# Tokens as the stationary side of the second product: a batch's 576 tokens as four blocks of 128, with 64 left over

## The chip, the cores and the metric

The kernel runs on one core of one Trainium2 chip. The core has TensorE (PE in the profile, its weight loads PEld), VectorE (DVE), ScalarE (ACT), GpSimd (POOL) and SyncE (SP), which here only issues transfers. The metric is device time in microseconds (us) of one execution, lower is better.

## The reference

Eight batches of 576 tokens. In each of 8 heads of 64, 32 learned positions `p` attend to the tokens, and the tokens then attend to what that packed. The heads side by side are `x` with 4608 rows of 512, and a two-layer network with a leaky activation follows:

```python
def _ref(q, k, v, p, w_in, w_out, alpha):
    p_packed = sm_attn(p, k, v)
    x = sm_attn(q, p_packed, p_packed)      # 4608 x 512, float32
    h = x @ w_in                            # 512 x 2048
    g = np.maximum(h, 0.0) + alpha * np.minimum(h, 0.0)
    return g @ w_out                        # 2048 x 512
```

## The kernel before

Everything is held transposed: features on the partitions, tokens along the columns. A number that must be exact is split into a high and a low part of type fp32r, and a product is made of three matmuls (high by high, high by low, low by high).

The hidden width 2048 is cut into `NF` = 16 slices `f` of 128. `pieces` lists stretches of tokens: half batches of 288 for batches 0 to 5, and for the last two batches 320, 512 (256 of each) and 320. For one piece `k` and one `f`:

- `first(k, f)` (lines 702 to 739) makes the hidden slice in PSUM, `ps_h`. From batch 1 on that is six matmuls of the piece's width (lines 724 to 726). The packed `w_in` of the batch comes from `split_pw`, which splits 256 columns at a time on ACT and POOL (lines 694, 695). Then the activation: ACT (731), DVE (732), and the split of the result into `gh` (ACT, 737) and `gl` (DVE, 738), two buffers each.
- `second(k, f)` (lines 741 to 786) multiplies by `w_out`. A 128 x 128 block of `w_out` is stationary and the piece's tokens move: 4 blocks of output features x 3 matmuls = 12 matmuls of the piece's width (line 757), into the accumulators `acc0` to `acc3`, one PSUM bank each. At `f` = 15 each bank is copied out by DVE or ACT (783, 781) and stored by SP (786).

The loop at the end of the kernel runs through `order`: at step i it calls `first` of entry i and `second` of entry i - 2 (`AHEAD` = 2). Between these it lets generators go on by a step: the attention of coming batches (lines 244 to 507), the conversion of the weights, and `packed_w` (642), which makes the packed `w_in` of a coming pair of batches, its weights loaded by SP into the three buffers of pool `win` (line 650). `plan` says from which step on each generator runs. Batches 0 and 1 go in sweeps over parts of `f` (`part`); from entry 64 on (batch 2) each piece runs through all 16 slices. A scheduler reorders instructions within what their data allow, so the order on an engine isn't that of the text. Attention with `hold` set would wait for a step; `2 * g - 2 >= 6` never holds with eight batches.

## Time and profile before

| | |
|---|---|
| median of 3 runs | 791.69 us (790.46, 791.77, 791.69) |
| span of the profiled execution, first to last instruction | 790.0 us (the profile gives no other time of it) |
| PE, PEld busy | 97%, 91% |
| ACT, DVE, POOL busy | 69%, 59%, 45% |
| TensorE's granted clock, by 40ths of the span | 9 tenths or more of full speed throughout |
| DMA | 91.68 MB, mean 116 GB/s |

Busy time of PE counts pipelined matmuls with modelled ends, so that two neighbours overlap: the cost of a matmul in a stream is the distance from its start to the next one's, which the timeline shows. Idle time of an engine that isn't the limit costs nothing.

### The profile page before, as it was taken

Reading aid. Unit: us, or ns where it says so; the run is one execution under the profiler, and the core shown is the slowest. Engines: PE = TensorE matmul, PEld = TensorE weight load, DVE = VectorE, ACT = ScalarE, POOL = GpSimd, SP = SyncE. Lnnn points to the kernel's source line nnn. Section 1 sums busy time; section 2 is a strip of 40 time slices with the busy share of each in tenths; the row PEclk is TensorE's granted clock in tenths of the full one; section 3 lists DMA queues with packets and bytes.
Section 4 is the critical chain, followed back from the end, with each engine's and each line's share of the span. In section 5 each row is a group of like instructions: output and inputs, shape, how many; then the busy total and the mean of one; then the engine's idle time right before and its main releaser. Section 6 shows DMA issues by size and latency. Waiting matters only on the chain.

```text
span 790.0 us, 14895 instructions
## 1 busy us (share of the span) xinstructions
PE 766.6 (97%) x5168; PEld 715.6 (91%) x5168; DVE 464.1 (59%) x1070; ACT 543.3 (69%) x1242; POOL 359.2 (45%) x391
## 2 busy tenths in 40 slices
PE   6789999999999999999999999999999999999998
PEld 4567668999999899999999999999999999988898
DVE  3989988776857435557654265576663343432433
ACT  4788789776777887677768776777678644534343
POOL 2003306563777755678764155676632222333220
PEclk9999999999999999999999999999999999999999
DMA  9787775121363774232225621321037100000100
GB/s 317 258 259 256 242 223 156 46 64 46 104 197 121 263 239 152 75 91 76 79 88 186 231 89 46 91 61 46 1 92 244 42 32 1 34 1 1 49 6 34
DMA packets 59035, 91.68 MB, mean 116 GB/s; under 512 B 5200, under 2 KB 35920, under 8 KB 58960
## 3 DMA queue, kind: packets, MB, share of 16 engines
q1 hardware_dynamic: 58384, 90.33, 35.9%
q8 instruction: 41, 0.67, 0.4%
q10 hardware_dynamic: 576, 0.40, 0.2%
q14 instruction: 34, 0.28, 0.1%
HBM read 68.69 MB, written 22.02 MB: 115 GB/s over the span
## 4 chain that ended last, share of the span: by engine, by line
PE 83%; ACT 8%; DVE 4%; DMA 3%; issue 1%; ACTq 0%; DVEq 0%; SPq 0%
PE acc L757 47%; PE ps_h L724 7%; PE ps_h L725 7%; PE ps_h L726 7%; PE ps_h L713 3%; DMA wraw<-in_w_in 2%; PE ps_m L386 2%; PE ps_m L224 2%; PE ps_m L225 2%; PE ps_m L673 1%; PE ps_m L671 1%; PE ps_m L672 1%; DVE mag L140 1%; ACT pw L639 1%; PE acc L215 1%
## 5 line engine op out<-in xcount | busy, mean ns | idle before, releaser
L757 PE MATMUL acc<-gh,wo 128*128 128x288 f32 (+2 forms) x1920 | 331.1, 306 | 3.1 <-ACT gh L737 2.9
L757 PEld LDWEIGHTS acc<-gh,wo 128*128 128x128 f32 x1920 | 283.3, 188 | 19.8 <-ACT gh L737 6.2
L695 POOL TENSOR_TENSOR pwl<-pw,pwh 128x512 fp32r<-128x512 f32 (+1 forms) x128 | 148.2, 1164 | 220.6 <-ACT pwh L694 155.6
L732 DVE SCALAR_TENSOR_TENSOR ps_h<-neg,nal,ps_h 128x288 f32<-128x288 f32 (+2 forms) x240 | 129.1, 539 | 156.2 <-ACT neg L731 155.3
L757 PE MATMUL acc<-gl,wo 128*128 128x288 f32 (+2 forms) x960 | 197.3, 308 | 0.0
L738 DVE TENSOR_TENSOR gl<-ps_h,gh 128x288 fp32r<-128x288 f32 (+2 forms) x240 | 113.7, 474 | 88.3 <-ACT gh L737 85.4
L757 PEld LDWEIGHTS acc<-gl,wo 128*128 128x128 f32 x960 | 150.5, 188 | 4.8
L737 ACT CAST gh<-ps_h 128x288 fp32r<-128x288 f32 (+2 forms) x240 | 99.7, 416 | 76.9 <-DVE ps_h L732 63.4
L724 PE MATMUL ps_h<-a_h,pwh 128*128 128x288 f32 (+2 forms) x448 | 133.7, 298 | 0.0
L725 PE MATMUL ps_h<-a_l,pwh 128*128 128x288 f32 (+2 forms) x448 | 132.3, 295 | 0.0
L726 PE MATMUL ps_h<-a_h,pwl 128*128 128x288 f32 (+2 forms) x448 | 132.3, 295 | 0.0
L731 ACT ACTIVATE neg<-ps_h 128x288 f32<-128x288 f32 (+2 forms) x240 | 102.3, 427 | 39.5 <-PE ps_h L726 31.0
L694 ACT CAST pwh<-pw 128x512 fp32r<-128x512 f32 (+1 forms) x128 | 70.8, 567 | 64.9 <-PE ps_h L725 62.0
L188 POOL TENSOR_TENSOR xl<-xraw,xh 128x576 fp32r<-128x576 f32 x48 | 69.8, 1457 | 51.1 <-ACT xh L187 44.3
L725 PEld LDWEIGHTS ps_h<-a_l,pwh 128*128 128x128 f32 x448 | 84.4, 188 | 1.3 <-issue 0.2
L724 PEld LDWEIGHTS ps_h<-a_h,pwh 128*128 128x128 f32 x448 | 84.3, 188 | 1.4 <-issue 0.2
L726 PEld LDWEIGHTS ps_h<-a_h,pwl 128*128 128x128 f32 x448 | 84.4, 188 | 0.2
L676 ACT COPY pw<-ps_m 64x512 f32<-64x512 f32 x96 | 55.7, 581 | 7.6 <-PE ps_m L673 6.0
L344 POOL TENSOR_TENSOR vs<-vraw,vs 128x640 fp32r<-128x640 f32 x24 | 37.7, 1573 | 10.7 <-ACT vs L343 8.3
L227 ACT COPY lo<-ps_m 64x288 f32<-64x288 f32 x96 | 37.3, 396 | 6.3 <-PE ps_m L225 4.4
L713 PE MATMUL ps_h<-a_f,pw 128*128 128x288 f32 x128 | 38.1, 420 | 3.1 <-DVE a_f L481 3.1
L187 ACT CAST xh<-xraw 128x576 fp32r<-128x576 f32 x48 | 32.1, 674 | 6.6 <-PE ps_m L224 3.5
(132 smaller groups left out, 920.5 us busy)
## 6 DMA issues: line engine op xcount, KB each, us to landing
w<-w_split SPq DMA_DIRECT2D x32, 512.0 KB, 4.1
xraw<-in_kT SPq DMA_DIRECT2D x32, 288.0 KB, 3.0
xraw<-in_qT SPq DMA_DIRECT2D x32, 288.0 KB, 2.8
vraw<-in_v SPq DMA_DIRECT2D x32, 256.0 KB, 2.9
wraw<-in_w_in SPq DMA_DIRECT2D x16, 512.0 KB, 5.0
wraw<-in_w_out SPq DMA_DIRECT2D x16, 512.0 KB, 4.4
w_split<-w SPq DMA_DIRECT2D x16, 512.0 KB, 2.9
w<-w_whole SPq DMA_DIRECT2D x24, 256.0 KB, 3.5
```

The costliest lines, as they stand in the source:

```text
L188: nc.gpsimd.tensor_tensor(out=xl, in0=raw, in1=fv(xh), op=ALU.subtract)
L694: nc.scalar.copy(out=th[:, w], in_=src)
L695: nc.gpsimd.tensor_tensor(out=tl[:, w], in0=src, in1=fv(th[:, w]), op=ALU.subtract)
L713: nc.tensor.matmul(ps[:, :size], th[:, i, fs], a_f[:, i, t : t + size], start=(i == 0), stop=(i == 1))
L724: nc.tensor.matmul(po, th[:, w, i], a_h[:, i, tok], start=hi, stop=False)
L725: nc.tensor.matmul(po, th[:, w, i], a_l[:, i, tok], start=False, stop=False)
L726: nc.tensor.matmul(po, tl[:, w, i], a_h[:, i, tok], start=False, stop=lo)
L731: nc.scalar.activation(out=neg, in_=x, func=AF.Relu, scale=-1.0)
L732: nc.vector.scalar_tensor_tensor(out=x, in0=neg, scalar=nal[:, f : f + 1], in1=x, op0=ALU.mult, op1=ALU.add)
L737: nc.scalar.copy(out=gh, in_=x)
L738: nc.vector.tensor_tensor(out=gl, in0=x, in1=fv(gh), op=ALU.subtract)
L757: product = nc.tensor.matmul(acc[o][:, :width], wo_t[f][:, half_, os_], g, start=begin and n == 0, stop=end and n == 2,)
```

## The change

Batches 0 and 1 stay as they are. From batch 2 on, `order` alternates between the two halves of a batch at each `f`, and `first` always makes 288 columns. In `second_by_tokens` the token side `g` is stationary (128 tokens) and all 512 columns of `w_out[f]` move: per half batch two blocks of 128 tokens, so 2 x 3 = 6 matmuls of 512 columns into two banks (`acc0`, `acc1` for the first half, `acc2`, `acc3` for the second). The 32 tokens that are left in each half are stored to DRAM (`g_rest`), for each `f` one transfer of 128 x 2 x 32 numbers; at the end of a pair of batches `rest` loads the pair's 128 left-over tokens (four loads of 512 KB into the buffers of `win`) and runs 48 matmuls of 512 columns, into `acc3` or, at the very end, a bank of `ps_m`. For the last four slices of the last batch the left-over tokens are put straight into the loaded tile by POOL.

The output now has tokens on the partitions. `put` turns a bank on DVE in blocks of 32 x 32 and stores it in four transfers of 32 x 16 pieces of 128 bytes. In the last batch `put_turned` copies a bank out (half by ACT, half by DVE), turns it with four PE transposes, copies it out again and stores it. The buffers of the output tile go from 4 to 3, `gh` and `gl` become one tile `g` with four buffers, and `split_pw` splits once per batch and not once per half or piece. `hold` goes away.

```diff
-    op = ctx.enter_context(tc.tile_pool(name="op", bufs=4))
+    op = ctx.enter_context(tc.tile_pool(name="op", bufs=3))
...
+    g_rest = [dram.tile([NJ, P, 4, 2, P], F32, name=f"g_rest{g}") for g in range(1, B // 2)]
...
-        ways = pieces[k]
-        n = 256 // len(ways)
-        h = f * P // n
-        if (k, h) not in pj:
...
+        b, h = k // 2, f // 2
+        own = (b, k % 2 if b < 2 else 0, h)
+        if own not in pj:
+            th = pwj.tile([P, 2, 256], F32R, name="pwh", tag="pwh")
+            tl = pwj.tile([P, 2, 256], F32R, name="pwl", tag="pwl")
+            j, c = h // 2, h % 2 * 256
+            src = pw[b, j][:, :, c : c + 256]
+            nc.scalar.copy(out=th, in_=src)
+            nc.gpsimd.tensor_tensor(out=tl, in0=src, in1=fv(th), op=ALU.subtract)
+            pj[own] = (th, tl)
+        fs = slice(f % 2 * P, f % 2 * P + P)
+        return [t[:, :, fs] for t in pj[own]]
...
-        for b, t, size in ways:
-            for half in range(t // HS, -(-(t + size) // HS)):
...
+        b, t = k // 2, k % 2 * HS
...
+        x = ps_h.tile([P, 512], F32, name="ps_h", tag="h")[:, :HS]
...
-        gh = gp.tile([P, width], F32R, name="gh", tag="gh")
-        gl = gp.tile([P, width], F32R, name="gl", tag="gl")
-        nc.scalar.copy(out=gh, in_=x)
-        nc.vector.tensor_tensor(out=gl, in0=x, in1=fv(gh), op=ALU.subtract)
-        gs[k, f] = (gh, gl)
+        g = gp.tile([P, 2, HS], F32R, name="g", tag="g", bufs=4)
+        nc.scalar.copy(out=g[:, 0], in_=x)
+        nc.vector.tensor_tensor(out=g[:, 1], in0=x, in1=fv(g[:, 0]), op=ALU.subtract)
+        gs[k, f] = g
...
-                nc.scalar.copy(out=part[k][:, o], in_=acc[o][:, :width])
+                nc.scalar.copy(out=part[k][:, o], in_=acc[o][:, :HS])
                 continue
-            if k in part:
-                to = part[k][:, o]
-            elif width > CW:
-                if o % 2 == 0:
-                    two = pwp.tile([P, 2, 512], F32, name="two", tag="pw")
-                to = two[:, o % 2]
...
+            nc.vector.tensor_tensor(out=to, in0=acc[o][:, :HS], in1=to, op=ALU.add)
+            if f == NF - 1:
+                nc.sync.dma_start(out=outT[o * P : (o + 1) * P, b * S + t : b * S + t + HS], in_=to)
+
+    def by_tokens(to, st, f, kept_order=False):
+
+        for n, (i, half_) in enumerate(((0, 0), (0, 1), (1, 0))):
+            product = nc.tensor.matmul(
+                to, st[:, i], wo_t[f][:, half_, :],
+                start=(f == 0 and n == 0), stop=(f == NF - 1 and n == 2),
+            )
+            if kept_order:
+                tc.keep_in_program_order(product)
+
+    def put(of, toks):
+
+        to = op.tile([P, DM], F32, name="ot", tag="ot")
+        nc.vector.transpose(out=to, in_=of)
+        for r, tok in enumerate(toks):
+            nc.sync.dma_start(
+                out=outT[:, tok : tok + 32].rearrange("(c j) i -> j c i", j=32),
+                in_=to[32 * r : 32 * r + 32].rearrange("j (c i) -> j c i", i=32),
+            )
...
+    def put_turned(of, runs, n):
+
+        tag = ("xh", "xl")[n % 2]
+        own = xin.tile([P, S], F32, name="own", tag=tag)[:, :DM].rearrange("t (q o) -> t q o", q=NOC)
+        nc.scalar.copy(out=own[:, : NOC // 2], in_=of[:, : DM // 2])
+        nc.vector.tensor_copy(out=own[:, NOC // 2 :], in_=of[:, DM // 2 :])
+        yield
+        turned = ps_h.tile([P, 512], F32, name="ps_h", tag="h").rearrange("o (q t) -> o q t", q=NOC)
+        to = op.tile([P, NOC, P], F32, name="ot", tag="ot")
+        for q in range(NOC):
+            tc.keep_in_program_order(nc.tensor.transpose(turned[:, q], own[:, q], ident))
+        nc.scalar.copy(out=to[:, : NOC // 2], in_=turned[:, : NOC // 2])
+        nc.vector.tensor_copy(out=to[:, NOC // 2 :], in_=turned[:, NOC // 2 :])
+        n = P // len(runs)
+        for i, tok in enumerate(runs):
+            nc.sync.dma_start(
+                out=outT.rearrange("(q o) t -> o q t", o=P)[:, :, tok : tok + n],
+                in_=to[:, :, i * n : i * n + n],
+            )
+        yield
...
+    def second_by_tokens(k, f):
+        b, hf = k // 2, k % 2
+        if f == 0:
+            for n in range(2):
+                tag = f"acc{2 * hf + n}"
+                acc_t[k, n] = ps_a.tile([P, 512], F32, name=tag, tag=tag)
+        g = gs.pop((k, f))
+        c0, r0 = ((0, 256), (32, 0))[hf]
+        own = slice((2 * (b % 2) + hf) * 32, (2 * (b % 2) + hf) * 32 + 32)
+        left_over = fv(g[:, :, r0 : r0 + 32])
+        if b == B - 1 and f >= NF - 4:
+            if not kept:
+                kept.append(win.tile([P, 4, 2, P], F32R, name="rest", tag="w"))
+                nc.sync.dma_start(
+                    out=fv(kept[0][:, :, :, : P // 2]), in_=g_rest[-1][NJ - 1, :, :, :, : P // 2]
+                )
+            nc.gpsimd.tensor_copy(out=kept[0][:, f % 4, :, own], in_=left_over)
+        else:
+            nc.sync.dma_start(out=g_rest[b // 2 - 1][f // 4, :, f % 4, :, own], in_=left_over)
+        for n in range(2):
+            by_tokens(acc_t[k, n], g[:, :, c0 + n * P : c0 + n * P + P], f, b == B - 1 and f == NF - 1)
+            if f == NF - 1:
+                at_ = b * S + hf * HS + c0 + n * P
+                if b == B - 1:
+                    turns.append(put_turned(acc_t.pop((k, n)), [at_], len(turns)))
+                    next(turns[-1])
+                else:
+                    put(acc_t.pop((k, n)), range(at_, at_ + P, 32))
...
+    def rest(bp, pool, tag):
+
+        to = pool.tile([P, 512], F32, name=f"rest_{tag}", tag=tag)
+        for j in range(NJ):
+            if j == NJ - 1 and kept:
+                st = kept[0]
...
+                st = win.tile([P, 4, 2, P], F32R, name="rest", tag="w")
+                nc.sync.dma_start(out=fv(st), in_=g_rest[bp - 1][j])
+            for f in range(4):
+                by_tokens(to, st[:, f], 4 * j + f, bool(kept) and j > 0)
+            if j == NJ - 1:
+                if kept:
+                    turns.append(put_turned(to, [(2 * bp + i) * S + 256 for i in range(2)], 0))
+                    next(turns[-1])
+                else:
+                    put(to, [(2 * bp + i) * S + 256 + r for i in range(2) for r in (0, 32)])
+            yield
...
-    order += [(k, f) for k in range(4, len(pieces)) for f in range(NF)]
+    order += [(2 * b + hf, f) for b in range(2, B) for f in range(NF) for hf in range(2)]
...
-            plan += [(T + at_n, attention(2 * g + n // 2, n % 2, hold=(None, T + HOLD[n % 2])[n // 2] if 2 * g - 2 >= 6 else None), RG)]
+            plan += [(T + at_n, attention(2 * g + n // 2, n % 2), RG)]
...
-        if i >= AHEAD:
-            second(*order[i - AHEAD])
+        if i < AHEAD:
+            continue
+        k, f = order[i - AHEAD]
+        if k < 4:
+            second(k, f)
+            continue
+        second_by_tokens(k, f)
+        if k % 4 != 3:
+            continue
+        if k < 2 * B - 1:
+            if f == NF - 1:
+                drain(rest(k // 4, ps_a, "acc3"))
+        elif f == NF - 1:
+            for _ in rest(k // 4, ps_m, "m"):
+                drain(turns.pop(0))
+            drain(turns.pop(0))
```

Three places of the program, as the builder orders them. PE first, in the middle of a batch: the second product of one step before (piece of 288; `acc` are the accumulators, `wo` is `w_out`), with the last matmul of the `ps_h` ahead of it and half of the next one behind it:

```order
L726 MATMUL ps_h_7982<-a_h_4980,pwl_7984 128x288
L757 MATMUL acc0_7848<-gl_7927,wo4_551 128x288
L757 MATMUL acc1_7849<-gl_7927,wo4_551 128x288
L757 MATMUL acc2_7850<-gl_7927,wo4_551 128x288
L757 MATMUL acc3_7851<-gl_7927,wo4_551 128x288
L757 MATMUL acc0_7848<-gh_7960,wo5_688 128x288 x2
L757 MATMUL acc1_7849<-gh_7960,wo5_688 128x288 x2
L757 MATMUL acc2_7850<-gh_7960,wo5_688 128x288 x2
L757 MATMUL acc3_7851<-gh_7960,wo5_688 128x288 x2
L724 MATMUL ps_h_8012<-a_h_4980,pwh_7983 128x288
L725 MATMUL ps_h_8012<-a_l_4981,pwh_7983 128x288
L726 MATMUL ps_h_8012<-a_h_4980,pwl_7984 128x288
```

and now, in the middle of batch 5, the end of one half's step and the beginning of the other's:

```order
L704 MATMUL ps_h_7842<-a_h_4705,pwl_7800 128x288
L749 MATMUL acc0_7159<-wo14_2164,g_7812 128x512
L749 MATMUL acc1_7160<-wo14_2164,g_7812 128x512
L749 MATMUL acc2_7195<-wo14_2164,g_7832 128x512 x2
L749 MATMUL acc3_7196<-wo14_2164,g_7832 128x512 x2
L702 MATMUL ps_h_7862<-a_h_4705,pwh_7799 128x288
L703 MATMUL ps_h_7862<-a_l_4706,pwh_7799 128x288
L704 MATMUL ps_h_7862<-a_h_4705,pwl_7800 128x288
```

12 matmuls of 288 columns became 6 of 512 (four with the high part of `g`, two with the low part of it, one `ps_h` later). The six of `ps_h` stay as they were, between the high part and the low one.

SP's queue where the last but one batch ends, before (the stores of the last three pieces and the last loads of `packed_w`):

```order
L650 DMA w_8480<-w_split_100 128x1024
L650 DMA w_8500<-w_split_100 128x1024
L786 DMA outT<-ot_8841 128x288
L786 DMA outT<-ot_8853 128x288
L786 DMA outT<-ot_8847 128x288
L786 DMA outT<-ot_8859 128x288
L786 DMA outT<-ot_9325 128x320
L786 DMA outT<-ot_9337 128x320
L786 DMA outT<-ot_9331 128x320
L786 DMA outT<-ot_9343 128x320
L786 DMA outT<-two_9929 128x512 x2
L786 DMA outT<-two_9940 128x512 x2
```

and now, from the end of batch 6 into batch 7 (`g_rest3` is the store of left-over tokens, `ot` the turned output):

```order
L805 DMA g_rest3_103<-g_8635 128x2x32
L761 DMA outT<-ot_8666 32x16x32 x4
L761 DMA outT<-ot_8675 32x16x32 x4
L761 DMA outT<-ot_8698 32x16x32 x4
L761 DMA outT<-ot_8707 32x16x32 x4
L805 DMA g_rest3_103<-g_8659 128x2x32
L805 DMA g_rest3_103<-g_8691 128x2x32
L805 DMA g_rest3_103<-g_8723 128x2x32
L805 DMA g_rest3_103<-g_8745 128x2x32
L800 DMA rest_9234<-g_rest3_103 128x8x64
```

Sixteen stores of output stand in a row, and the left-over stores of the next batch's first steps are behind them; the load of a part of `rest` follows.

PE at the very end, before:

```order
L757 MATMUL acc0_9966<-gh_10328,wo15_2420 128x320 x2
L757 MATMUL acc0_9966<-gl_10329,wo15_2420 128x320
L757 MATMUL acc1_9967<-gh_10328,wo15_2420 128x320 x2
L757 MATMUL acc1_9967<-gl_10329,wo15_2420 128x320
L757 MATMUL acc2_9968<-gh_10328,wo15_2420 128x320 x2
L757 MATMUL acc2_9968<-gl_10329,wo15_2420 128x320
L757 MATMUL acc3_9969<-gh_10328,wo15_2420 128x320 x2
L757 MATMUL acc3_9969<-gl_10329,wo15_2420 128x320
```

and now (`rest_m` is the sum of the left-over tokens, `own` a bank copied out to be turned):

```order
L749 MATMUL rest_m_9373<-wo11_1529,rest_9420 128x512 x3
L776 MATMUL ps_h_9434<-ident_107,own_9364 128x128 x4
L749 MATMUL rest_m_9373<-wo12_1731,rest_9234 128x512 x3
L749 MATMUL rest_m_9373<-wo13_1942,rest_9234 128x512 x3
L749 MATMUL rest_m_9373<-wo14_2164,rest_9234 128x512 x3
L749 MATMUL rest_m_9373<-wo15_2382,rest_9234 128x512 x3
L776 MATMUL ps_h_9458<-ident_107,own_9370 128x128 x4
L776 MATMUL ps_h_9467<-ident_107,own_9455 128x128 x4
```

The last accumulating matmuls are those of the left-over tokens, and two groups of four transposes follow them.

## Rows read from the trace of the kernel before

**Rows 1.** Windows: length, busy us (count) of PE, PEld, DVE, ACT, POOL, clock, DMA
```profile
0.00:268.00 268.00, 248.16 (x1522) 211.50 (x1523) 205.73 (x482) 206.34 (x477) 115.31 (x135) 0.99 0.56 179
268.00:455.00 187.00, 186.99 (x1365) 183.58 (x1364) 99.81 (x246) 144.40 (x326) 111.07 (x117) 1.00 0.46 143
455.00:636.00 181.00, 180.95 (x1336) 178.53 (x1335) 99.46 (x243) 127.45 (x294) 91.78 (x95) 1.00 0.24 76
636.00:787.00 151.00, 150.52 (x952) 141.97 (x950) 59.09 (x102) 65.10 (x148) 41.06 (x46) 1.00 0.05 17
```

**Rows 2.** Who waited for whom, weight loads, 268 to 787 us: us, times, longest
```profile
PEld acc L757 <- ACT gh L737: 0.5, 2, 0.3
```

**Rows 3.** Timeline of PE: start, us, engine, line; second product, 288 columns
```profile
499.88 0.43 PE L757 MATMUL acc<-gh,wo 128*128 128x288 f32 x2
...
501.08 0.43 PE L757 MATMUL acc<-gh,wo 128*128 128x288 f32 x2
```

**Rows 4.** Timeline of PE: last twelve of 256 columns, then 512
```profile
713.56 0.28 PE L724 MATMUL ps_h<-a_h,pwh 128*128 128x256 f32 x1
...
715.00 0.39 PE L757 MATMUL acc<-gh,wo 128*128 128x512 f32 x1
...
715.92 0.40 PE L757 MATMUL acc<-gl,wo 128*128 128x512 f32 x1
```

**Rows 5.** Chain of waits: start and length of stretches, batches 6 and 7
```profile
657.01 1.76 PE acc L757 x12
659.65 1.76 PE acc L757 x12
...
706.74 4.40 PE acc L757 x19
...
715.16 4.40 PE acc L757 x19
```

**Rows 6.** Timeline of PE: transposes of 128 by 128
```profile
355.57 0.71 PE L363 MATMUL ps_m<-ident,s_t 128*128 128x128 f32 x5
```

**Rows 7.** Timeline of all engines: the end
```profile
786.21 0.31 PE L757 MATMUL acc<-gl,wo 128*128 128x320 f32 x1
786.59 0.42 ACT L781 COPY ot<-acc 128x320 f32<-128x320 f32 x1 [0.48 <-PE acc L757]
...
787.04 0.35 ACTq L786 DMA_DIRECT2D outT<-ot  x1
```

**Rows 8.** DMA issues: count, KB each, us to landing
```profile
w<-w_split SPq DMA_DIRECT2D x32, 512.0 KB, 4.1
...
outT<-ot SPq DMA_DIRECT2D x32, 144.0 KB, 1.9
```

**Rows 9.** One line, L560, stores in 512 pieces: SP ns min/median/max; landing
```profile
L560 SPq DMA_DIRECT2D w_whole<-w x4: 377/384/386, 14.6 to 40.9; - x4
...
DMA to landing us min/median/max: 3.6/4.3/5.4
```

**Rows 10.** Groups by line, DVE, 268 to 787 us: count, busy us, mean ns, idle before
```profile
L732 DVE SCALAR_TENSOR_TENSOR ps_h<-neg,nal,ps_h 128x288 f32<-128x288 f32 (+2 forms) x175 | 95.8, 548 | 141.7 <-ACT neg L731 141.0
L738 DVE TENSOR_TENSOR gl<-ps_h,gh 128x288 fp32r<-128x288 f32 (+2 forms) x175 | 84.4, 482 | 75.4 <-ACT gh L737 73.3 <-PE ps_h L726 0.9 <-PE ps_h L725 0.5
...
L504 DVE STREAM_TRANSPOSE s<-t 128x576 f32<-128x576 f32 x8 | 6.2, 777 | 1.0 <-POOL t L499 1.0
```

**Rows 11.** Groups by line, ACT, 268 to 787 us
```profile
L731 ACT ACTIVATE neg<-ps_h 128x288 f32<-128x288 f32 (+2 forms) x174 | 75.0, 431 | 30.5 <-PE ps_h L726 29.3
L737 ACT CAST gh<-ps_h 128x288 fp32r<-128x288 f32 (+2 forms) x175 | 73.7, 421 | 64.1 <-DVE ps_h L732 52.2 <-PE acc L757 10.6
```

**Rows 12.** Waits of the SP queue, 268 to 787 us: us, times, longest
```profile
SPq L181 <- POOL xl L188: 98.4, 24, 10.7
```

**Rows 13.** Timeline around an eviction: DVE
```profile
358.38 0.81 DVE L783 COPY ot<-acc 128x288 f32<-128x288 f32 x2
```

**Rows 14.** Timeline around the same eviction: the SP queue
```profile
358.86 1.87 SPq L786 DMA_DIRECT2D outT<-ot  x4
```

More of the change, by code (lines that the diff above doesn't have):

```diff
@@ L371, in attention @@
                 )
-        if hold is None:
-            q0 = load_x(qT, b, pr0)
+        q0 = load_x(qT, b, pr0)
         yield
@@ L776, in second @@
-            if k in part:
-                nc.vector.tensor_tensor(
-                    out=to, in0=acc[o][:, :width], in1=part[k][:, o], op=ALU.add
-                )
-            elif o % 2:
-                nc.scalar.copy(out=to, in_=acc[o][:, :width])
-            else:
-                nc.vector.tensor_copy(out=to, in_=acc[o][:, :width])
-            if f == NF - 1:
-                queue = nc.scalar if o % 2 and k == len(pieces) - 1 else nc.sync
-                queue.dma_start(out=outT[o * P : (o + 1) * P, b * S + t : b * S + t + width], in_=to)
@@ L788, in pack_attention_ffn_kernel @@
-    pieces = [[(k // 2, k % 2 * HS, HS)] for k in range(4)]
-    for b in range(2, B, 2):
-        if b < 6:
-            pieces += [[(c, hf * HS, HS)] for c in (b, b + 1) for hf in range(2)]
-        else:
-            pieces += [[(b, 0, CW)], [(b, CW, S - CW), (b + 1, 0, S - CW)], [(b + 1, S - CW, CW)]]
-    result, pw, pj, gs, acc, part = {}, {}, {}, {}, [], {}
-    done, owner, clock = set(), {}, [0]
+            to = part[k][:, o]
+            nc.vector.tensor_tensor(out=to, in0=acc[o][:, :HS], in1=to, op=ALU.add)
@@ L798, in pack_attention_ffn_kernel @@
+    result, pw, pj, gs, acc, acc_t, part, kept, turns = {}, {}, {}, {}, [], {}, {}, [], []
+    done, owner = set(), {}
     later = []
```

80 lines of the change are left out of this document (22 added, 58 removed).

## The prediction

> **What bounds the kernel now.** I read the windows by stage first. They say which engine is full, and where. From 268 us on (batch 2 begins; the 268 us ahead of that run code that stays) PE is busy for 187.0 of 187.0, 181.0 of 181.0 and 150.5 of 151.0 us, at a granted clock of 1.00, which is the 2.4 GHz level; ACT, DVE and POOL are busy for 77% at most [rows 1]. The waits come next, since a busy share alone doesn't tell whether PE starves: over these 519 us its weight loads waited 0.5 us for another engine [rows 2]. So the later stage is as long as PE's stream of matmuls, and a change there is worth what it takes out of that stream, as long as nothing new makes PE wait. Making ACT or POOL lighter is worth nothing.
>
> What a matmul costs in a stream is read from starts in the timeline. Nine of 288 columns take 501.08 - 499.88 = 1.20 us, 0.133 us each [rows 3]. Twelve of 256 take 715.00 - 713.56 = 1.44 us, 0.120 each; then four of 512 take 0.92 us, 0.230 each [rows 4]. The chain checks this over a longer stretch: two slices of the 512 piece take 715.16 - 706.74 = 8.42 us, which is 4.21 for 12 of 256 and 12 of 512, so that one of 512 costs (4.21 - 1.44) / 12 = 0.231 [rows 4, 5]. A slice of a 320 piece (18 matmuls) takes 659.65 - 657.01 = 2.64 us [rows 5].
>
> **Second product, batches 2 to 5.** Per step (half a batch, one slice) 12 x 0.133 = 1.60 us become 6 x 0.231 = 1.39 us, and the left-over tokens add 48 matmuls per 64 steps, 0.75 x 0.231 = 0.17. The columns are equal, 3456 on both sides; what falls is the number of matmuls, 12 to 6.75, and with it a small cost of each. That is 1.60 - 1.56 = 0.04 us a step, with unrounded values 0.041; times 128 steps **-5.2 us**. Bounds: 0.230 for 512 columns makes it -6.0; 0.1330 for 288 makes it -4.7.
>
> By the Trainium skill (TensorE: Matmul & The Clock Gate, Back-to-back issue gap) a warm matmul costs its columns at 2.4 GHz and about 2.5 ns, 122.5 and 215.8 ns here. By that the step would save 0.013 us and the stage 1.7 us. The rows are longer by 11 and 15 ns, and they decide: -5.2.
>
> **Batches 6 and 7.** Before, a slice of both batches took 2 x 2.64 + 4.21 = 9.49 us [rows 5]. After, it is 24 x 0.133 in the first product and 27 x 0.231 in the second, 9.44. Over 16 slices **-0.8 us**. Against it PE turns five banks, 20 transposes; five in a row take 0.71 us [rows 6], 0.14 each. Sixteen of them lie in the stream: **+2.3 us** (a little less if the next matmul starts before the last one's end).
>
> **The end.** Before: the last matmul ends at 786.52, a copy of 0.42 us, a store issued at 787.04 and landed 1.9 later, and about 1 us of closing, to 790.0 [rows 7, 8]. After, the last sum is copied out (0.34 us by columns), turned by four transposes (up to 0.71), copied again (0.34), and stored by two transfers from one queue, the second 0.35 later. That replaces one copy of 0.42: 0.34 + 0.71 + 0.34 + 0.35 - 0.42, and two handovers of 0.07 [rows 6, 7]: **+1.5 us**. The four transposes are in it.
>
> **What is hidden.** Splitting once per batch removes 64 of the 112 pairs of operations that `split_pw` issues on ACT and POOL in this stage; no wait of PE hangs on them [rows 2], so 0. The removed `hold` never held: 0. Of evictions, 44 copies on DVE and ACT go, and 22 turns on DVE come, 0.777 x 512/576 = 0.69 us each [rows 10]: 15 us more on an engine with over 40% free [rows 1]. On SP's queue 184 left-over stores, 94 stores of output instead of 44 and 12 loads come, at 0.34 to 0.39 us each [rows 7, 9] some 90 us of 519 together (246 more transfers). These would cost only by coming late, and that is priced at two places.
>
> First, **the end of a batch** (five times). Put zero where the first half's two banks are full. DVE turns one by 0.75; its four stores are issued 0.385 apart [rows 9], the fourth at 1.9. With three output buffers, the turn of the fourth bank waits until they have landed; then 0.69 and a handover. PE wants that bank again after 15 matmuls of 512 and three `first` of 0.80, counted in the order between those points: at 5.9 us (at the first pair's end, where other work is put between, at 13). So a store may take 3.2 us to land. Output stores took 1.9 [rows 8], the only ones in 512 pieces 3.6 to 5.4, while the DMA was fuller than here [rows 1, 9]. I take a value nearer to 1.9, because the DMA is idle for half the time or more from 268 us on: **0**. The ends stay for the range.
>
> Second, **the buffers of `g`**. A left-over store reads `g`, and its buffer is written anew four steps later, 4 x (0.80 + 1.39) = 8.8 us. The low part (0.48), issue (0.34) and landing (1.9) use 2.7 of that [rows 8, 10], so SP may run 6 us late before ACT waits. PE has another 1 us: behind a `first` the order gives it 2.65 us of other matmuls before it uses the high part, and the chain to that takes 0.43 + 0.55 + 0.42 us and three handovers [rows 10, 11]. At a batch's end the sixteen output stores ahead take 16 x 0.385 = 6.2 us, which just fits. A load that waits in SP's queue ahead of a store is the danger: loads of `xraw` waited for POOL 24 times for 4.1 us in the mean, 10.7 at most [rows 12]. But SP had little else to do then, and where a store stood in the queue it came on time: two copies ran from 358.38 to 359.19, and the first store was issued at 358.86, just past half way, when the first of them was done [rows 13, 14]. I take **0**, bounds 0 and +5. The loads of `rest` stand behind the sixteen stores at the end of the first pair: these are out by about 7.5, a load lands 4.1 later [rows 8], and the order puts 13 us of matmuls ahead of its use; 0 too.
>
> **The sum.** -5.2 - 0.8 + 2.3 + 1.5 = -2.2. The profiled execution has a span of 790.0, so 787.8; the median of the three runs lies 1.69 above that span, and I leave that as it is: **789.5 us**. About 0.2%, 1.6 us, is what a measurement of this kernel can tell from no change; so "faster" means below 790.1, "slower" above 793.3.
>
> **Rivals.**
>
> *Short pieces land late* (slower). Before, this stage stores pieces of 1152 bytes or more; now of 128. If a store takes 3.6 us, the fourth bank is 0.4 late at each of five ends, 2 us in all; at 4.3 it is 1.1 and 5.5, so 795.0; at 5.4 it is 2.2 and 11, 800.5. DVE stands still in that wait, and the left-over stores slip behind it. It decides from a landing of 3.2 us on. For it: [rows 9]. Against it: [rows 8]. The Trainium skill (DMA: Bandwidth & Descriptors, Specifications) speaks for it: below 512 bytes a transfer is a read-modify-write. No transfer that this trace shows by line stores so little at a time. Chance 0.14, 793.3 to 802.
>
> *Left-over stores behind late loads* (no change). Two to five waits of 7 to 10 us ahead of a store would each stall PE by about 1 us, or the loads of `rest` by 1 to 2 us twice: 790.5 to 793. For it: the waits of 10.7 us [rows 12]. Against it: stores on time [rows 13, 14]. Chance 0.24.
>
> *Only the columns count* (slower). The columns are equal before and after. If a matmul cost nothing beside them, both gains would be 0, and the transposes and the end would leave 791.69 + 2.3 + 1.5 = 795.5. Against it: by the rows, 256 columns more cost 0.231 - 0.120 = 0.111 us, so 256 alone should cost 0.111, not 0.120 [rows 4, 5]. The skill's rule above lies between, at 793.0. Chance 0.02.
>
> *More goes than counted.* PE's half microsecond of waits [rows 2], 0.230 for 512, transposes at 0.11: 787.3 to 788. It is the lower end of the forecast.
>
> **How the numbers follow.** The forecast's case has 0.60, nearly all below 790.1, and its own range is 787.3 to 790.3. Faster 0.58; same 0.26 (the case of no change and a little of the forecast's); slower 0.16. The range is 787.3 to 794.2: it leaves out a few per cent below and most of the late landings.
>
> **What the profile will show.** Right: matmuls of 512 columns 0.230 to 0.232 us apart with `g` stationary, PE's waits from 268 us on below 2 us, the first stage as it was, output stores landing in under 3 us, and the last accumulating matmul about 3.5 us earlier than 786.2, with an end that is longer by 1.5. Wrong: weight loads waiting for ACT's cast of `g` (buffers), matmuls into `acc3` waiting for DVE's turn at the ends of batches, a landing over 3.2 us, or a distance of more than 0.233 us.

## Result and profile after the change

796.97 us, median of 4 runs (795.29 to 798.09), beside 791.62 for the kernel before on the same chip: ratio 1.0066, 95% interval 1.0048 to 1.0083. It is slower by 5.35 us; I had forecast 789.5, and a range that ended at 794.2. The profiled execution of the change took 798.09 us with a span of 796.2, so its span lies 6.2 us above the one shown before.

The windows of the changed kernel, in the stretches of [rows 1] and with the same columns:

```profile
0.00:268.00 268.00, 250.12 (x1525) 212.47 (x1526) 206.31 (x483) 207.17 (x479) 115.66 (x135) 0.99 0.57 179
268.00:455.00 187.00, 183.52 (x1024) 159.77 (x1023) 105.72 (x258) 139.06 (x313) 93.16 (x102) 1.00 0.58 155
455.00:636.00 181.00, 180.45 (x998) 157.29 (x997) 100.13 (x237) 114.48 (x264) 69.94 (x78) 1.00 0.43 109
636.00:787.00 151.00, 150.62 (x808) 130.50 (x807) 64.11 (x131) 57.28 (x139) 18.65 (x21) 1.00 0.20 40
```

The first 268 us are as they were, and so is the clock. From 268 to 455 us PE now has 3.5 us without work; DVE gained 6 us of work there and ACT lost 5. From 268 us on ACT, DVE and POOL are busy for 75% at most, and yet PE waits. The waits of PE's weight loads from 268 us on, which came to 0.5 us before [rows 2]:

```profile
PEld acc L749 <- ACT g L712: 5.2, 10, 0.8
PEld rest_acc L749 <- DMA rest<-g_rest: 2.2, 1, 2.2
PEld ps_h L702 <- DVE g L713: 1.3, 4, 0.7
PEld acc L749 <- DVE den L330: 0.7, 1, 0.7
```

Two things stand out: ACT's cast of `g` (L712) comes late ten times, and one load of `rest` comes 2.2 us late.

**The balance.** From the starts of all matmuls of the two traces, from 266 us to the last one that accumulates, I added the distance to the next start that belongs to each in an undisturbed stream (0.133 us for 288 columns, 0.231 for 512, 0.120 for 256, and so on), and apart from that whatever a start came later than so. The distances fall from 518.4 to 513.4 us, the rest rises from 1.8 to 10.5, and from the end of the last accumulating matmul to the end of the span 3.4 us became 5.8. That is -5.0 + 8.7 + 2.4 = 6.1 of the 6.2 us. The gain came; 8.7 us of waiting, of which I had priced nothing, came with it.

**An end of a batch: two turns ahead of a sum.** The timeline around the end of batch 5, first of DVE, then of ACT, then of PE:

```profile
623.83 0.46 DVE L713 TENSOR_TENSOR g<-ps_h,g 128x288 fp32r<-128x288 f32 x1 [0.47 <-ACT g L712]
624.42 1.31 DVE L759 STREAM_TRANSPOSE ot<-acc 128x512 f32<-128x512 f32 x2
625.66 0.48 DVE L708 SCALAR_TENSOR_TENSOR ps_h<-neg,nal,ps_h 128x288 f32<-128x288 f32 x1
626.62 0.72 DVE L759 STREAM_TRANSPOSE ot<-acc 128x512 f32<-128x512 f32 x1 [0.47 <-PE acc L749]
```
```profile
624.25 0.41 ACT L707 ACTIVATE neg<-ps_h 128x288 f32<-128x288 f32 x1 [0.46 <-PE ps_h L704]
626.44 0.41 ACT L707 ACTIVATE neg<-ps_h 128x288 f32<-128x288 f32 x1 [1.78 <-PE ps_h L704]
626.75 0.39 ACT L712 CAST g<-ps_h 128x288 fp32r<-128x288 f32 x1
```
```profile
623.99 1.55 PE L749 MATMUL acc<-wo,g 128*128 128x512 f32 x6
626.18 0.63 PE L749 MATMUL acc<-wo,g 128*128 128x512 f32 x2
627.19 1.20 PE L749 MATMUL acc<-wo,g 128*128 128x512 f32 x4 [0.38 <-ACT g L712]
```

The sum of the activation (L708) could begin at 624.66, when ACT's `neg` is there. It begins at 625.66, behind two turns that stand together, 1.31 us. Its result comes at 626.1; by then ACT has the next `neg` ahead of the cast in its order, so the cast starts at 626.75 instead of some 625.2, and PE, which wants `g` at 626.6, goes on at 627.19: 0.55 us lost. By the same rows a cast ahead of that `neg` could have started at 626.2 and ended at 626.6, when PE wants it; that order was not tried. The same piece comes again at 708 (0.55 us), and at 351 (0.33) a turn stands ahead of the sum too: 1.4 us in this trace. At 355 PE loses 0.39 us because the fourth bank's turn waits for an output buffer. Not every late cast is of this kind: at 482 no turn is near, and ACT has work of the attention ahead of the cast.

```profile
481.58 0.78 ACT L324 ACTIVATE s_t<-s_t,nmx 128x576 f32<-128x576 f32 x1
...
482.35 0.38 ACT L712 CAST g<-ps_h 128x288 fp32r<-128x288 f32 x1
```

PE loses 0.24 us there, and 0.26 at 543 and 0.47 at 297, where other work of ACT stands ahead of the cast too. At 450 it loses 0.59 us though nothing stands in the way: `neg`, sum and cast take from 449.21 to 450.61, 1.4 us, and PE's order leaves 1.0 us of other matmuls for them. The six matmuls of the first PE row above give the distance: (1.55 - 0.39) / 5 = 0.232, as forecast.

**The first pair's end: SP's queue.** The timeline of the SP queue, then the two parts of the chain of waits (start, length) and the PE rows there:

```profile
439.30 9.80 SPq L761 DMA_DIRECT2D outT<-ot  x15
449.20 1.39 SPq L824 DMA_DIRECT2D rest<-g_rest  x3
450.68 2.72 SPq L805 DMA_DIRECT2D g_rest<-g  x4
```
```profile
440.69 4.25 DMA outT<-ot
...
449.20 5.05 DMA rest<-g_rest
```
```profile
452.04 0.40 PE L749 MATMUL acc<-wo,g 128*128 128x512 f32 x1
454.29 0.96 PE L749 MATMUL rest_acc<-wo,rest 128*128 128x512 f32 x3 [1.85 <-DMA rest<-g_rest]
```

The first of the sixteen output stores goes out at 438.4; the loads of `rest` stand behind the last one and go out from 449.20 on, 10.8 us later (I had priced 7.5); the first lands 5.05 later (priced 4.1); and PE stands for 2.0 us. The store that holds the chain from 440.69 is one that the fourth turn waited for, since there are three output buffers: PE lost another 0.7 us at 445. At the end of batch 5 no load stood between the stores; there the sixteen take 8.56 us. What an issue costs SP, and the landing, by line:

```profile
625.16 8.56 SPq L761 DMA_DIRECT2D outT<-ot  x16
```
```profile
L761 SPq DMA_DIRECT2D outT<-ot x88: 337/490/1744, 349.8 to 715.0; - x88
...
DMA to landing us min/median/max: 1.7/1.9/4.9
```

The landing is the 1.9 us that I took, but only in the median: at the first pair's end, behind loads of w of 512 KB, the store issued at 439.30 landed 4.9 us later, the one at 440.69 4.25. The issue is not what I took either: 0.337 us when a store goes alone, 0.49 in the median, and 0.54 from one to the next in a row of them, against the 0.385 that I read from [rows 9].

**The end.** PE's last product, then the copies by ACT and DVE:

```profile
787.30 3.04 PE L749 MATMUL rest_m<-wo,rest 128*128 128x512 f32 x12
...
790.38 0.37 ACT L770 COPY own<-rest_m 128x256 f32<-128x256 f32 x1 [2.42 <-PE rest_m L749]
790.78 0.42 DVE L771 COPY own<-rest_m 128x256 f32<-128x256 f32 x1 [2.37 <-ACT own L770]
...
791.74 0.37 ACT L777 COPY ot<-ps_h 128x256 f32<-128x256 f32 x1 [0.55 <-PE ps_h L776]
792.14 0.42 DVE L778 COPY ot<-ps_h 128x256 f32<-128x256 f32 x1 [0.50 <-ACT ot L777]
```

The two halves of each copy don't run side by side: DVE's starts when ACT's has ended, and the profile names ACT's as what it waited for. A copy takes 0.37 + 0.03 + 0.42 = 0.82 us and not 0.34, twice, which makes the end 2.4 us longer and not 1.5.

### The profile page after: what moved, and what is told of

Read it like the earlier page. It is cut to its first block, busy times and chain, and to the rows that moved or that the text cites. A ratio compares the mean times of both kernels' runs of the same rounds, so it can differ in the third digit from the quotient of the medians.

```text
span 796.2 us, 13773 instructions
## 1 busy us (share of the span) xinstructions
PE 769.4 (97%) x4372; PEld 663.4 (83%) x4372; DVE 478.0 (60%) x1112; ACT 519.5 (65%) x1198; POOL 297.4 (37%) x335
## 4 chain that ended last, share of the span: by engine, by line
PE 75%; ACT 9%; DMA 7%; DVE 6%; issue 2%; SPq 1%; POOL 0%; ACTq 0%; DVEq 0%
PE acc L749 31%; PE acc L732 7%; PE ps_h L702 7%; PE ps_h L704 7%; PE ps_h L703 7%; DMA wraw<-in_w_in 3%; PE rest_acc L749 3%; PE ps_h L697 2%; PE ps_m L385 1%; PE ps_m L224 1%; PE rest_m L749 1%; PE ps_m L225 1%; DVE mag L140 1%; PE ps_m L660 1%; PE ps_m L662 1%
## 5 line engine op out<-in xcount | busy, mean ns | idle before, releaser
L749 PE MATMUL acc<-wo,g 128*128 128x512 f32 x1152 | 313.9, 396 | 2.1 <-ACT g L712 1.7
L749 PEld LDWEIGHTS acc<-wo,g 128*128 128x128 f32 x1152 | 202.7, 188 | 35.1 <-ACT g L712 5.2
L708 DVE SCALAR_TENSOR_TENSOR ps_h<-neg,nal,ps_h 128x288 f32<-128x288 f32 x256 | 132.0, 517 | 131.7 <-ACT neg L707 130.3
L713 DVE TENSOR_TENSOR g<-ps_h,g 128x288 fp32r<-128x288 f32 x256 | 115.8, 453 | 92.3 <-ACT g L712 88.4
L707 ACT ACTIVATE neg<-ps_h 128x288 f32<-128x288 f32 x256 | 105.3, 412 | 87.6 <-PE ps_h L704 80.8
L712 ACT CAST g<-ps_h 128x288 fp32r<-128x288 f32 x256 | 102.1, 400 | 91.7 <-DVE ps_h L708 83.0
L702 PE MATMUL ps_h<-a_h,pwh 128*128 128x288 f32 x448 | 134.1, 299 | 0.5 <-DVE g L713 0.5
L703 PE MATMUL ps_h<-a_l,pwh 128*128 128x288 f32 x448 | 132.2, 295 | 0.0
L704 PE MATMUL ps_h<-a_h,pwl 128*128 128x288 f32 x448 | 132.0, 295 | 0.0
L732 PE MATMUL acc<-g,wo 128*128 128x288 f32 x768 | 127.7, 307 | 3.1 <-ACT g L712 3.1
L732 PEld LDWEIGHTS acc<-g,wo 128*128 128x128 f32 x768 | 109.3, 188 | 14.6 <-ACT g L712 5.8
```

The costliest lines, as they stand in the source:

```text
L702: nc.tensor.matmul(x, th[:, i], a_h[:, i, tok], start=(i == 0), stop=False)
L703: nc.tensor.matmul(x, th[:, i], a_l[:, i, tok], start=False, stop=False)
L704: nc.tensor.matmul(x, tl[:, i], a_h[:, i, tok], start=False, stop=(i == 1))
L707: nc.scalar.activation(out=neg, in_=x, func=AF.Relu, scale=-1.0)
L708: nc.vector.scalar_tensor_tensor(out=x, in0=neg, scalar=nal[:, f : f + 1], in1=x, op0=ALU.mult, op1=ALU.add)
L712: nc.scalar.copy(out=g[:, 0], in_=x)
```

## Experiments

My theory after this reading: the 8.7 us lie at the ends of batches, and have two sources, the place of DVE's turns and SP's queue behind sixteen output stores. The rivals: DVE's turns alone, by their length; left-over stores and the buffers of `g` throughout; the DMA, filled by 128-byte pieces; the pitch (the distance of two matmuls) or the end. All runs are listed here; the last column is PE's time beyond the distances from 266 us on, counted as above in the one profiled execution of each run. Executions of one kernel lie 1 to 5 us to either side of their median, so this column and the median can differ by as much. The runs come from several chips, so two of them are best compared by their ratios, each to the kernel before on its own chip.

| run | median us | ratio to before, 95% | beyond, us |
|---|---|---|---|
| before | 791.3 to 791.9 | | 1.8 |
| the change | 796.97 | 1.0048 to 1.0083 | 10.5 |
| x5 the change again | 797.34 | 1.0049 to 1.0088 | 9.9 |
| x1 loads of `rest` early | 797.22 | 1.0042 to 1.0085 | 7.9 |
| x2 one store of four | 796.22 | 1.0030 to 1.0066 | 7.9 |
| x3 that, turns of 128 | 792.25 | 0.9985 to 1.0020 | 4.3 |
| x13 as x2, turn behind the sum | 793.19 | 1.0008 to 1.0038 | 5.2 |
| x6 turn behind the sum | 799.75 | 1.0075 to 1.0114 | 12.2 |
| x4 stores in two queues | 802.95 | 1.0101 to 1.0175 | 15.5 |
| x9 pieces of 512 bytes | 802.94 | 1.0134 to 1.0169 | 14.6 |
| x10 that, turn behind the sum | 805.09 | 1.0145 to 1.0197 | 14.1 |
| x14 four `ot`, three `g` | 804.37 | 1.0136 to 1.0173 | 16.8 |
| x7 last pair as before | 796.32 | 1.0037 to 1.0085 | 10.3 |
| x8 turns, loads, last pair | 796.94 | 1.0042 to 1.0081 | 8.0 |
| x11 pieces of 256 bytes | 793.41 | 1.0014 to 1.0032 | 6.2 |
| x12 pieces, loads, last pair | 791.02 | 0.9988 to 1.0007 | 4.9 |

**x1, the loads of `rest` ahead of the stores.**

```diff
+        if k % 4 == 3 and k < 2 * B - 1 and f == NF - 1:
+            for j in range(3):
+                load_rest(k // 4, j)
         second_by_tokens(k, f)
```

> The change, with the first three loads of `rest` put into SP's queue ahead of the sixteen output stores of a pair's end (batches 2 to 5), not behind them. My theory (time goes at the ends of batches; there the stores take 16 x 0.54 = 8.6 us of SP's queue, and the loads behind them make PE wait 2.0 us once): the wait of `rest_acc` on its load goes from 2.0 to under 0.3 us and the rest stays, 794.5 to 795.5 us. Rival A (left-over stores and buffers of g hold PE throughout, not SP's queue at the ends): 796.5 to 797.5. Rival B (nothing of the stalls is DMA, all is DVE's turns): the wait shrinks in the trace but another takes its place, 796 to 797.5.

797.22 us: no gain in the median, though in its profile the wait for `rest` is 1.2 us instead of 2.2 and PE's time beyond the distances 2.6 less. The interval leaves anything from no gain to some 2 us; this run settles nothing. The loads now stood among the stores in SP's queue, not ahead of all of them.

**x2, one store of four; x3, with turns of 128 columns.**

```diff
-        for r, tok in enumerate(toks):
+        for r, tok in list(enumerate(toks))[:1]:
```
```diff
-        nc.vector.transpose(out=to, in_=of)
+        nc.vector.transpose(out=to[:, :P], in_=of[:, :P])
```

> The change, with one of the four output stores of each bank issued and three left out in batches 2 to 6 (three quarters of those outputs are not written); DVE's turns stay. My theory: SP's burst at a batch's end falls from 8.6 to about 2.1 us, so the wait for `rest` (2.0) and the fourth turn's wait for an output buffer (0.8 on DVE, about 1.2 us on PE at the first pair's end) go; the waits of 0.5 to 0.65 us for ACT's cast of g behind two turns stay: 793 to 794.5 us. Rival A (left-over stores and buffers of g hold PE throughout): under 1 us less, 796 to 797. Rival B (all is DVE's turns): no less, 796.5 to 797.5. Rival C (the pitch of 512 columns or the end is longer than I read): no less, and the stalls would not add up.

> As the run with one store of four, and DVE turns only 128 of a bank's 512 columns, and stores only these, in batches 2 to 6 (fifteen sixteenths of those outputs are not written): 20 turns of about 0.2 us instead of 0.72. My theory: the casts of g come on time at the ends of batches, 5 times 0.5 to 0.9 us less than with whole turns: 789.5 to 791.5 us, and PE's waits from 268 us on below 3 us in all. Rival S (the stores make the stalls, the turns are hidden): the same as the run with whole turns, 793 to 794.5. Rival C (pitch or end): 795 or more.

Without three quarters of the stores the time falls by less than I expected: 796.22 lies where the rival of the left-over stores has it. In its profile it is 2.6 us less beyond the distances, but that execution was the fastest of ten (793.46). With short turns as well (0.31 us each instead of 0.72) it falls by 4.0 to 792.25, a little above what I expected, and the waits of 0.5 us at 620 and 700 us are gone. The stores of x3 are smaller too, a quarter of x2's bytes. So the turns carry the larger part, by their length or by their place, if those smaller stores don't; x6 and x13 look at the place.

**x4, every second store in ACT's queue.**

```diff
-            nc.sync.dma_start(
+            (nc.sync, nc.scalar)[r % 2].dma_start(
```

> The change, with every second output store of batches 2 to 6 in ACT's queue instead of SP's, nothing left out. My theory: SP's burst falls from 8.6 to 4.3 us, so the wait for `rest` goes (2.0 us less), while ACT, which makes g, has 8 issues per end: if one holds ACT for 0.1 us or less the time is 794 to 795.5; if it holds ACT for as long as SP (0.5 us), five ends of 4 us make g late and it is 797 to 801. Rival B (all is DVE's turns): 796 to 797.5.

802.95 us. An issue holds ACT for 0.372 us, and the store waits in ACT's order for DVE's turn. The last of its bounds holds, and 2 us beyond: relieving SP at ACT's cost is a loss, since ACT makes `g`.

**x5, the change again; x6, the second turn behind the sum.** In x6 the second turn of each two banks is tied behind L708 in DVE's order; no turn is shorter.

```diff
-        nc.vector.transpose(out=to, in_=of)
+        turn = nc.vector.transpose(out=to, in_=of)
+        if behind is not None:
+            tc.add_manual_dep(
+                turn.ins, behind.ins.name,
+                mybir.DependencyInfo(mybir.DependencyClass.NoSync, mybir.DependencyReason.DATA),
+                reason="keep_in_program_order",
+            )
```

> The change as it is, once more, beside the runs that follow and with a second profile. All theories: 796 to 798 us. If the load of `rest` that PE waits for at the first pair's end (2.0 us) comes with the program's order, the second profile shows that wait again at 1.5 to 2.5 us; if it is chance, it shows it below 0.5 us.

> The change, with one thing other: the second turn of each pair of banks must stand behind the next sum of the activation (L708) in DVE's order, so that DVE goes turn, sum, turn and not turn, turn, sum. Nothing is left out and no turn is shorter. My theory as the last runs leave it (DVE's two turns in a row, 1.4 us, hold up the sum, ACT's cast of g comes late, PE waits 0.5 to 0.9 us at each of five ends): these waits fall to under 0.2 us each, 793 to 795 us. Rival L (the turns' length counts, wherever they stand: the banks come free later and PE waits for DVE at acc1 or acc3): no less, 796 to 798. Rival S (the run with turns of 128 columns was faster for its small stores): no less, 796 to 798.

The second profile of the change has the wait for `rest` again, 1.6 us: it comes with the program's order. x6 came out at 799.75, against my theory on the face of it. Its waits of PE's weight loads say why:

```profile
PEld rest_acc L749 <- DMA rest<-g_rest: 3.4, 1, 3.4
PEld acc L749 <- ACT g L712: 2.6, 6, 0.8
```

The late casts fell from 5.2 to 2.6 us, and the pieces at 543, 627 and 708 us are gone (one of 0.56 is new at 719). But the wait for `rest` grew to 3.4: at the first pair's end SP issued a store for 3.6 us at one place, and its loads went out at 452.1. Two effects had met in one run, so x13 took SP's burst away first.

**x13, one store of four and the second turn behind the sum.**

> As the run with one output store of four in batches 2 to 6 (796.2 us; three quarters of those outputs are not written), and the second turn of each pair of banks behind the next sum of the activation; turns of full length. Now SP's queue is short, so the wait for `rest` can't take the gain back. If the order of the turns costs (turn, turn, sum): 793 to 794.5 us and no wait above 0.3 us at 480, 540, 620 and 700 us. If only their length does: 795.5 to 797, and shorter turns alone brought the 792.3.

793.19 us beside 796.22 with the same stores and turns, turns as long: with SP's queue short, the place of the turns alone is worth 3.0 us by the medians and 2.0 by the ratios (1.0048 and 1.0023; the two runs are on different chips, and their intervals overlap a little). DVE at the same place as above:

```profile
619.71 0.71 DVE L759 STREAM_TRANSPOSE ot<-acc 128x512 f32<-128x512 f32 x1
620.34 0.48 DVE L708 SCALAR_TENSOR_TENSOR ps_h<-neg,nal,ps_h 128x288 f32<-128x288 f32 x1
620.73 0.70 DVE L759 STREAM_TRANSPOSE ot<-acc 128x512 f32<-128x512 f32 x1
621.36 0.42 DVE L713 TENSOR_TENSOR g<-ps_h,g 128x288 fp32r<-128x288 f32 x1
```

Turn, sum, turn, low part: the sum waits for one turn and the second turn fills the time of ACT's cast. One wait that I had expected to go stayed, 0.74 us at 480, as in x3: it is the kind that the change has at 482, with ACT's work for the attention ahead of the cast. Shorter turns (x3) give 0.9 us more by the medians and 1.6 by the ratios, with intervals that overlap; whether their length costs too stays open.

**x9, pieces of 512 bytes; x10, with the turn behind the sum.** The same bytes and as many stores, each in 128 pieces of 512 bytes instead of 512 of 128.

```diff
+            own = outT[:, toks[0] : toks[0] + P].rearrange("(p q) t -> p q t", q=4)
+            for r in range(4):
+                rows = slice(32 * r, 32 * r + 32)
+                nc.sync.dma_start(out=own[rows], in_=to[rows].rearrange("j (q t) -> j q t", q=4))
```

> The change, with the same bytes of each bank of batches 2 to 6 stored by as many stores, but in pieces of 512 bytes and not of 128 (these outputs come to stand in a wrong order; the banks of left-over tokens stay as they are). Turns and their order stay. Theory D (1 MB in pieces of 128 bytes fills the DMA at the end of a pair for over 8 us, at 120 to 130 GB/s, and the loads of `rest` share it): issue of a store below 0.4 us, the wait for `rest` below 0.5 us instead of 1.6 to 2.0, the fourth turn without a wait for its buffer; the waits behind two turns in a row stay: 793.5 to 795.5 us. Rival Q (each issue holds SP for 0.5 us whatever its pieces): issue 0.49 as before, 796 to 798. Rival DVE alone: 796 to 798.

> The same with pieces of 512 bytes, and the second turn of each pair of banks behind the next sum of the activation. By the last runs the turn's place took away the waits of 0.25 to 0.55 us at four ends, and lost more at the first pair's end, where the wait for `rest` grew to 3.3 us. If that loss was the DMA's, both gains now show: 791 to 793 us, PE's waits beside the pitch from 266 us on below 6 us. If later turns cost for themselves (rival L): 795 or more.

802.94 and 805.09 us, the opposite of what theory D expects; and with the longer row of stores the turn behind the sum gained nothing, as in x6. The DMA had a quarter of the packets to carry, and its mean busy share at batch 6's end was 0.40 (709 to 720 us) instead of 0.66 (707 to 716 in the change); but by the line's own view each issue now held SP longer, the first of a row too:

```profile
L764 SPq DMA_DIRECT2D outT<-ot x80: 570/598/698, 350.6 to 719.1; - x80
```

Sixteen take 10.3 us instead of 8.5. At batch 6's end the left-over stores (L811 in this kernel) stand behind them on the SP queue, and ACT's cast waits for one of these on ACT:

```profile
709.40 10.30 SPq L764 DMA_DIRECT2D outT<-ot  x16
719.81 2.09 SPq L811 DMA_DIRECT2D g_rest<-g  x4
```
```profile
721.62 0.92 ACT L712 CAST g<-ps_h 128x288 fp32r<-128x288 f32 x2 [1.10 <-DMA g_rest<-g]
```

PE lost 1.76 us there, 1.59 at 364 and 2.09 at the wait for `rest`. So what costs is how long SP is held by a row of stores, not how full the DMA is; 1.8 us more in each row cost 6 us in all. Why such a store takes 0.6 us to issue, no run shows.

**x14, four output buffers, three of `g`.**

```diff
-    op = ctx.enter_context(tc.tile_pool(name="op", bufs=3))
+    op = ctx.enter_context(tc.tile_pool(name="op", bufs=4))
-        g = gp.tile([P, 2, HS], F32R, name="g", tag="g", bufs=4)
+        g = gp.tile([P, 2, HS], F32R, name="g", tag="g", bufs=3)
```

> The change with four output buffers instead of three and three of g instead of four. If the fourth turn's wait for a buffer at the first pair's end (0.8 us on DVE, about 1 us on PE there) counts: that wait goes, 795.5 to 796.5 us, unless three buffers of g make ACT's cast wait for left-over stores (behind sixteen output stores, 0.5 to 2 us at several ends): then 798 to 803 us, with waits of `acc` on the cast after each burst.

804.37 us, the second bound. DVE no longer waits for an output buffer (3.1 us once in x5's profile, none here), but with one buffer of `g` less the cast waits longer for left-over stores, and PE for the cast:

```profile
ACT g L712 <- DMA g_rest<-g: 7.1, 5, 3.0
```
```profile
PEld acc L749 <- ACT g L712: 6.7, 10, 1.8
PEld rest_acc L749 <- DMA rest<-g_rest: 3.1, 1, 3.1
```

In the change itself, with four buffers, ACT waited like this twice, 5.8 us in all, at places where PE had other matmuls:

```profile
ACT g L712 <- DMA g_rest<-g: 5.8, 2, 4.4
```

By these waits it is the same mechanism as x9's, reached from the other side: a longer row of stores, or less room to bear it.

**x7, the last pair as in batches 0 and 1; x8, with x6 and x1.** In x7 `second` (w_out stationary, 288 columns) does batches 6 and 7, each bank copied out and stored.

> The change in batches 2 to 5 alone; batches 6 and 7 with w_out stationary and 288 columns of g moving, as batches 0 and 1 are done, a copy and a store at the end. My terms: end -1.5, sixteen transposes -2.3, the columns of two batches 16 x (4 x 18 x 0.133 - 9.44) = +2.2, the waits at batch 6's end and between the last transposes -1.0: together -2.6, 794 to 795 us. Rival (the end and the transposes cost nothing beside what the ends of batches cost): 797 to 799.

> The turns behind the sums, the loads of `rest` ahead of the output stores, and batches 6 and 7 with w_out stationary, together. My theory: -2 to -4 by the turns, -2.6 by the last pair, 0 to -2 by the loads (their own run did not show the 2 us in its median): 789 to 792 us, and from 268 us on PE waits for under 3 us. Rival L (length of the turns): 793 to 795.

796.32 and 796.94 us. The end is 1.6 us shorter in x7's profile (4.28 behind the last matmul instead of 5.85), but a new wait of 1.7 us stands at 717, for ACT's copy of a fourth bank into one of three output buffers: it starts at 718.63, and the first bank's store had landed at 718.49. In x8 the wait for `rest` is still 1.7 us. Neither gain showed, and I had not priced the buffer.

**x11, pieces of 256 bytes; x12, with the last pair and the early loads.** Nothing is left out. A bank takes every second of 256 tokens, two banks' turns interleave in one buffer, and eight stores go where sixteen went; the second turn stands behind the sum; `g` has three buffers, and the output two of twice the size. In x12 the last pair is done as in x7, copied out to free tiles of `pwp`.

```diff
+                st = g[:, :, c0 + n : c0 + 256 : 2]
...
+                    if n == 0:
+                        two = op.tile([P, 16, 32, 2], F32, name="two", tag="ot")
+                    turn = nc.vector.transpose(out=two[:, :, :, n], in_=acc_t.pop((k, n)).rearrange("p (c i) -> p c i", i=32))
...
...
+                            out=outT[:, at_r : at_r + 64].rearrange("(c j) i -> j c i", j=32),
```

> Nothing left out: each bank of batches 2 to 6 takes every second token, the turns of two banks interleave in one buffer, and eight stores of a batch carry pieces of 256 bytes instead of sixteen of 128; the second turn behind the sum; three buffers of g for four, to make room. Theory D: half the packets, half the time of the DMA at the ends: 792.5 to 795 us. Against it: three buffers of g leave one step less for the left-over store, which would show as ACT's cast waiting for DMA, 797 or more; or a stationary tile read with a stride of two loads slower than its 512 columns move, which would show in the distance of the matmuls, 800 or more.

> The pieces of 256 bytes, the loads of `rest` ahead of the stores of a pair's end, and batches 6 and 7 with w_out stationary, their sums copied out to tiles that `pw` has left free (with three output buffers PE waited 1.7 us there). Nothing is left out. Theory D and the turns: -3 to -4, the last pair -2 to -3: 789 to 792 us, which could be even with the kernel before or a little under it. If it stays at 795 or above, the gains of the single edits do not add, and something else holds PE at the ends.

793.41 and 791.02 us. The store of twice the bytes holds SP for 0.507 us (the line's own view of x11), so the row is half as long:

```profile
L833 SPq DMA_DIRECT2D outT<-two x40: 316/507/1090, 351.2 to 707.4; - x40
```

and in x12 (where the accumulating matmul is L763 and the cast L713) PE's weight loads wait for

```profile
PEld acc L763 <- ACT g L713: 1.5, 4, 0.5
PEld rest_acc L763 <- DMA rest<-g_rest: 0.6, 1, 0.6
```

In x11 PE still loses 1.5 us at 709, where the cast waits for a left-over store. x12, which has no left-over stores in the last pair, loses no more than 0.42 us at any place; the version is even with the kernel before (0.9988 to 1.0007) and doesn't beat it. Which part of x11 and x12 brings how much was not taken apart. A stationary tile with a stride of two costs nothing that shows in the distances.

## Why the prediction was wrong

- *Second product and batches 6 and 7*, -5.2 and -0.8: right. Of the -5.0 us of distances, twelve transposes in the stream make +1.1 to +1.3, so the columns gave some -6.2; in the second profile of the change the same count gives some -5.1 (some records of matmuls are missing, and such time goes to the other column). By the formula of the Trainium skill (TensorE: Matmul & The Clock Gate, Back-to-back issue gap), which the page gives for an isolated matmul, 512 columns take an estimated 0.2158 us; here they took 0.231 to 0.232, and the rows decide again. By that formula batches 6 and 7 would save an estimated 0.4 us, so the 793.0 that I set beside it should have been 793.4.
- *The transposes*, +2.3: half of it. Twelve and not sixteen lay in the stream, four of them in 0.35 us (786.95 to 787.30), 0.09 each; one bank's four fall into the end.
- *The end*, +1.5: +2.4. The term for the two halved copies was too small, 0.34 for what took 0.82 us, because the halves run one behind the other.
- *What is hidden*, DVE's turns: this is the step that failed. "15 us more on an engine with over 40% free" is a sum over 519 us. The turns come two in a row, four in some 5 us, ahead of the sum on which ACT's cast and PE hang. I had priced their lateness for the banks, not for the sum behind them. Their place was worth 2.0 to 3.0 us once SP's queue was short (x2 to x13); in the change's own trace the three waits with a turn ahead of the sum make 1.4.
- *The end of a batch*, 0: the landing that I had made the point of decision was 1.9 us in the median, as I took it. It passed my 3.2 us at the first pair's end alone (3.9 to 4.9 us); there the fourth turn waited, and PE lost 0.7 us. But in x2, with a quarter of the stores, one landed after 5.3 us at the same place, so the number of pieces doesn't explain it; both times a load of 512 KB had gone out just ahead. By the Trainium skill (DMA: Bandwidth & Descriptors, Specifications) a transfer below 512 bytes is a read-modify-write; in the median pieces of 128 bytes landed in 1.9 us and pieces of 512 in 2.1, so no run shows a cost of it in the landing. What failed is the 0.385 us an issue: I read it from four stores that went alone, and it was 0.54 in a row of sixteen.
- *The buffers of `g`* and *the loads of `rest`*, 0: the sixteen stores that "just fit" by 6.2 us took 8.6, and 10.8 us at the first pair's end, where a load of w stood between and one issue took 1.74 us. This is the second step that failed. The loads of `rest` came 2 us late as the second rival had it (790.5 to 793 us), which was right in kind, though not by late loads of `xraw`; I had counted it twice, and it came once. The buffers of `g` held: ACT waited 5.8 us for them, and PE lost nothing that I can tell. That x9 and x14, with a longer row or one buffer less, lose 6 and 7 us shows how near to the edge the change runs.

Of the 8.7 us, the change's own trace gives 3.1 to SP's queue (`rest` and the output buffers at 355 and 445 us), 1.4 to the turns ahead of the sum, and 1.6 to casts that come late without a turn (x13 still has 1.2 of that kind); some 2.6 us lie in pieces below 0.15 us that I can't assign. The two sources hang together, and no single edit that leaves all outputs in place gained anything clear of noise: the turn's place lost time in x6 and gained nothing in x10, where SP's row of stores was long, and gained in x13, where it was short. What the single edits on SP's queue are worth stays less certain than the turns: x2's median fell by 0.8 us only, its ratio by 1.4, its profile by 2.6.

The second set of runs of the change (x5) gives the same time, so the miss is not chance. Of the signs that I had named as wrong, weight loads waiting for ACT's cast of `g` came, for the turns and ACT's own work and not for the buffers, and so did landings over 3.2 us.

## What to carry to other kernels

Work that is added to an engine with free time costs by where it stands, not by its sum: look at what is queued behind it in the five microseconds in which it comes, and put a short instruction that others wait for ahead of long ones that are needed later. A row of DMA issues is a row of work for the issuing queue; take the time of an issue from a row as long as yours, and look what stands behind it. When an edit that should help makes things worse, ask what it met: x6 lost time, and the same edit gained in x13, once the queue beside it was short.

## What was not expected of the hardware

- Issuing a store took SP 0.337 us in the median when it stood alone or among few (x2), 0.418 with a quarter of those bytes and pieces (x3), 0.49 in a row with pieces of 128 bytes, 0.507 with 256 bytes and twice the data, and 0.598 with 512 bytes, alone or not. It follows neither the bytes nor the number of pieces.
- A turn of 128 by 128 took 0.312 us, of 128 by 512 0.717: by these two, 0.18 us of each doesn't depend on the columns, so cutting turns up is dear.
- Copies of two halves of one bank, by ACT and DVE, ran one after the other at the end (0.37 and 0.42 us).
